# Column-normalised attention followed by a top-1 mixture of experts: three spare half units behind a run-time branch

## The chip, the cores and the metric

The kernel runs on one core of a Trainium2 chip. The metric is the device time of one execution in microseconds (us), as the median of several runs. A separate execution under the hardware profiler gives the trace from which all rows below come. The engines are TensorE (PE; its weight loads are listed apart as PEld), VectorE (DVE), ScalarE (ACT), GpSimd (POOL) and SyncE (SP); POOL issues the indirect DMAs here and SP the direct ones. A `q` behind an engine's name (POOLq) is its sequencer.

## What is computed

For each of 4 batches `q`, `k`, `v` are 5056 x 256. The columns of `q` and `k` are normalised over the 5056 rows, a 256 x 256 matrix is formed from them and put through a softmax, and `v` is multiplied with it. The 20,224 rows that result are the tokens of a mixture of 8 experts with one expert for each token:

```python
qn = q / (norm(q, axis=1) + 1e-6);  kn = k / (norm(k, axis=1) + 1e-6)
a = softmax(kn.transpose(0, 2, 1) @ qn / tau)
x = (v @ a).reshape(B * S, D)
e_idx = argmax(x @ w_gate, axis=1)
for e in range(E):
    mask = e_idx == e
    h = maximum(x[mask] @ w1[e], 0)
    out[mask] = gate_w[mask] * eom[mask, e] * (h @ w2[e])
```

How many tokens each expert gets is known only at run time.

## The kernel before

**Stages.** `gram` (L306) builds the 256 x 256 matrix of a batch, `mix` (L434) multiplies `v` with it, `route` (L494) finds each token's expert and scatters the token into that expert's region of a DRAM buffer `xs_d`, and `blocks` (L895) runs the experts' two layers over units of rows gathered from `xs_d`. `prep` and `split` (L236, L260) write each expert's weights to DRAM as a high and a low float16 part (`wsc`), from which units fetch them. These generators are woven into one another by `_beside` (L27); the instruction order on each engine follows from that order and from the framework's scheduler.

**Units.** A full unit has 256 rows (`BLK`, `nt = 2`), a half unit 128 (`nt = 1`). All units have rows of one expert. The number of units is fixed when the kernel is built (L77 to L86): `EARLY` = 10 full units from the first three batches, `LATER` = 62 more full ones, and `NHALF` = 21 halves, which is what the worst split of the tokens over the experts needs; `NUNIT` = 93. Before the first 10 and before the other 83, `checkpoint` (L724) has DVE work out from the counts which expert and which rows each unit has: `table` (L614) writes them into `elist`, `used` (1 where the unit has rows) and `gi` (the gather's indices), `weights` (L681) writes `wi`, the index by which a unit fetches weights. A unit without rows gathers 128 filler rows whose output index lies out of bounds, so that its store moves nothing; its `wi` is out of bounds too. Its matrix work is done all the same, since the instructions are the same for any data.

**Order of the units.** 10 early full units, then `lead` = `LATER` - `NHALF` = 41 full ones (units 10 to 50), then 21 pairs of a full unit and a half (units 51 to 92). So half number h is unit 52 + 2h, and the last three halves are units 88, 90 and 92, with full units 87, 89 and 91 between them. Halves are filled from the front: those without rows are the last.

**A step of `blocks`.** In step g the first layer of unit g (`h_part`, L837: for each half of a quarter 6 matmuls, 48 in all, with 256 columns for a full unit and 128 for a half) alternates with the second layer of unit g-1 (`y_part`, L860: 48 matmuls of 256 columns for a full unit, 24 for a half), in quarters h0 y0 h1 y1 h2 y2 h3 y3. After a quarter of h, ACT (L854) and DVE (L855) make its float16 parts; after the last quarter of y, ACT scales the result (L879) into `yo`. POOL fetches the two weight matrices into `wbuf[0]` and `wbuf[1]` (`fetch_w`, L768), each of which has two buffers that units take in turn (`u % NW`), gathers rows (`fetch_x`, L781) up to 6 units ahead, and stores one row block of 128 per instruction (`store`, L885). `prepare` (L792) scales and splits the rows on DVE and ACT and transposes them by a DMA on SP (L831). Two units that follow each other in the same buffer with the same expert need no new weights: `wi` is then out of bounds.

**End.** After the last step comes `store(NUNIT - 1)`; what the framework adds behind it (drains and semaphores) has L982.

Of the kernel before, what the change touches and what calls it, by code (L numbers as in the profile page):

```python
# [13 lines left out]
I32 = mybir.dt.int32  # L14
# [7 lines left out]
BLK = 256  # L22
# [4 lines left out]
def _beside(main, *others):  # L27

    due = [0.0 for _ in others]
    for _ in main:  # L30
        for i, (gen, rate) in enumerate(others):
            due[i] += rate
            while due[i] >= 1.0:
                due[i] -= 1.0
                next(gen, None)
# [3 lines left out]
def tile_colnorm_attention_then_top1_moe(  # L39
# [12 lines left out]
    nc = tc.nc  # L52
    B, N, C = q.shape
    E = w_gate.shape[1]
    FF = w1.shape[2]
    NTOK = B * N
# [20 lines left out]
    EARLY = 10  # L77
    LATER = (NTOK - E * (BLK - 1) + BLK - 1) // BLK - EARLY
    NHALF = (NTOK - (EARLY + LATER) * BLK + E * (BLK // 2 - 1)) // (BLK // 2)
# [4 lines left out]
    FIRST = [-(-r * SURE // E) for r in range(E)]  # L84
    assert EARLY <= FIRST[2] and EARLY + LATER - NHALF >= FIRST[E - 1]
    NUNIT = EARLY + LATER + NHALF  # L86
    QM = max(LATER, NHALF)
    NW = 2

    cst = ctx.enter_context(tc.tile_pool(name="cst", bufs=1))  # L90
# [32 lines left out]
    units = []  # L123
# [16 lines left out]
    def iota_f(shape, pattern, base, mult, name):  # L140
        ti = one.tile([P, shape], I32, tag="iota_i", name=name + "_i")
        nc.gpsimd.iota(ti, pattern=pattern, base=base, channel_multiplier=mult)
        tf = cst.tile([P, shape], F32, name=name)
        nc.vector.tensor_copy(tf, ti)
        return tf
# [8 lines left out]
    eoff = iota_f(E, [[CAP, E]], 0, 0, "eoff")  # L154
    jf = iota_f(QM, [[1, QM]], 0, 0, "jf")
    real = cst.tile([P, 1], F32, name="real")
# [32 lines left out]
    ri = cst.tile([P, E], I32, name="ri")  # L189
    elist = cst.tile([P, NW + NUNIT], F32, name="elist")  # L190
    nc.vector.memset(elist, -1.0)
# [11 lines left out]
    def grouped(ins, group, why):  # L203
        tc.declare_no_dep(ins.ins, group=group, reason=why)
        tc.add_to_no_dep_group(group, ins.ins)
# [30 lines left out]
    def prep(first, end, tag):  # L236
        todo = []
        for r in range(first, end):
            for half in range(2):
                if tag == "st":  # L240
                    raw = wk.tile([P, R, CW], F32, tag="st", name=f"raw{r}_{half}", bufs=STB)
                    raw = raw.rearrange("p r w -> p (r w)")[:, :HW1]
                else:
                    raw = big.tile([P, HW1], F32, tag="raw", name=f"raw{r}_{half}", bufs=3)
                nc.gpsimd.indirect_dma_start(
                    out=raw,
                    out_offset=None,
                    in_=wraw[half],
                    in_offset=bass.IndirectOffsetOnAxis(ap=ri[:, r : r + 1], axis=0),
                    bounds_check=E * P - 1,  # L250
                    oob_is_err=False,
                )
                todo.append(lambda raw=raw, half=half, r=r: split(raw, half, r))
                yield
                if len(todo) > 1:
                    yield from todo.pop(0)()
        for f in todo:
            yield from f()
# [171 lines left out]
    def finish(gen):  # L430
        for _ in gen or ():
            pass
# [137 lines left out]
    def open_marks(ck):  # L570
        nc.gpsimd.dma_start(mark[:, ck : ck + 1], xs_d[NSLOT:, 0:1])
# [37 lines left out]

    gi = cst.tile([P, NUNIT], I32, name="gi")  # L610
    wi = cst.tile([P, NUNIT], I32, name="wi")
    used = cst.tile([P, NUNIT], F32, name="used")

    def table(ck, unit, Q, places):  # L614

# [65 lines left out]
    def weights(a, b):  # L681

        ok = sm.tile([P, NUNIT], F32, tag="tb_ok", name="tb_ok")[:, a:b]
        now = elist[:, NW + a : NW + b]
        nc.vector.tensor_tensor(out=ok, in0=now, in1=elist[:, a:b], op=ALU.is_equal)
        nc.vector.tensor_tensor(out=ok, in0=ok, in1=used[:, a:b], op=ALU.is_ge)
        row = sm.tile([P, NUNIT], F32, tag="tb_wt", name="tb_wt")[:, a:b]
        nc.vector.tensor_scalar(out=row, in0=now, scalar1=float(P), scalar2=pidx, op0=ALU.mult, op1=ALU.add)
# [4 lines left out]
    def of_rank(dst, src):  # L693
        pr = sm.tile([P, E, E], F32, tag="tb_rk", name="tb_rk")
        nc.vector.tensor_tensor(out=pr, in0=rank, in1=src.unsqueeze(1).to_broadcast([P, E, E]), op=ALU.mult)
        nc.vector.tensor_reduce(out=dst, in_=pr, axis=AX.X, op=ALU.add)
# [27 lines left out]
    def checkpoint(last):  # L724
        if last:
            close_regions()
        else:
            rank_experts()
        of_rank(rcr, rc)
        open_marks(int(last))  # L730
        yield
        if not last:
            table(int(last), BLK, EARLY, lambda a: [(a[:, :EARLY], lambda r: r)])
            weights(0, EARLY)
            new = [2] * EARLY
        else:

            s = 1
            lead = LATER - s * NHALF
            mid = EARLY + lead  # L740

            def fulls(a):
                grid = a[:, mid:].rearrange("p (h s) -> p h s", s=s + 1)
                return [
                    (a[:, EARLY:mid], lambda r: r[:, :lead]),
                    (grid[:, :, :s], lambda r: r[:, lead:].rearrange("p (h s) -> p h s", s=s)),
                ][not lead :]

            def halves(a):
                grid = a[:, mid:].rearrange("p (h s) -> p h s", s=s + 1)  # L750
                return [(grid[:, :, s], lambda r: r)]

            table(int(last), BLK, LATER, fulls)
            table(int(last), BLK // 2, NHALF, halves)
            weights(EARLY, NUNIT)
            new = [2] * lead + ([2] * s + [1]) * NHALF
        for nt in new:
            u = len(units)
            units.append(dict(nt=nt, gi=gi[:, u : u + 1], wi=wi[:, u : u + 1], top=max(r for r in range(E) if FIRST[r] <= u)))
# [5 lines left out]
    def fetch_w(half, u):  # L765
        end = (units[u]["top"] + 1) * P
        assert len(prepped) * P >= end
        nc.gpsimd.indirect_dma_start(  # L768
            out=wbuf[half][:, u % NW, :],
            out_offset=None,  # L770
            in_=wsc[half][:end, :],
            in_offset=bass.IndirectOffsetOnAxis(ap=units[u]["wi"], axis=0),
            bounds_check=end - 1,
            oob_is_err=False,
        )
# [106 lines left out]
    def store(u):  # L882
        un = units[u]
        for t in range(un["nt"]):
            ins = nc.gpsimd.indirect_dma_start(  # L885
                out=out[:, :],
                out_offset=bass.IndirectOffsetOnAxis(ap=un["id"][:, t : t + 1], axis=0),
                in_=un["yo"][:, t, :],
                in_offset=None,
                bounds_check=NTOK - 1,  # L890
                oob_is_err=False,
            )
            grouped(ins, "out", "each token has an output row of its own")

    def blocks():  # L895

        got = dict.fromkeys(("w1", "w2", "x", "prep"), 0)

        def adv(stage, step, n):
            for u in range(got[stage], min(n, len(units))):  # L900
                step(u)
                got[stage] = u + 1

        g = 0
        while g <= NUNIT:
            while g < NUNIT and g + 1 > len(units):
                yield
            adv("w1", lambda u: fetch_w(0, u), g + NW - 1 if g else NW)
            adv("w2", lambda u: fetch_w(1, u), g + NW - 1)
            adv("x", fetch_x, got["prep"] + QKB)  # L910
            if g > 1:
                store(g - 2)
            if g == 0:
                yield
            adv("prep", prepare, g + 1)
            if g < NUNIT:
                hb = big.tile([P, HW1], F32, tag="raw", name="hb", bufs=3)
                units[g]["h"] = hb.bitcast(F16).rearrange("p (a f m) -> p a f m", a=2, f=FC)
            for fp, steps in enumerate(ORDER):
                for kind, part in steps:  # L920
                    if kind == "h" and g < NUNIT:
                        h_part(g, part)
                    if kind == "y" and g > 0:
                        y_part(g - 1, part)
                if fp == 1:
                    adv("prep", prepare, g + 1 + XP)
                yield
            g += 1
        store(NUNIT - 1)


    grams = [gram(b) for b in range(B)]
# [3 lines left out]
    for _ in grams[0]:  # L936
        for _ in range(PER_STAGE):
            next(ahead)
    run = blocks()
    for b in range(B - 1):  # L940
        _beside(mix(b), (ahead, GRATE))
    early = checkpoint(False)
# [11 lines left out]
    _beside(tail, (run, BRATE))  # L954
    finish(checkpoint(True))
    _beside(run, (prep(2, E, "st"), WRATE))


# [28 lines left out]
```

## Time and profile before

| what | value |
|---|---|
| median of 3 runs | 1265.51 us (1261.57 to 1273.47) |
| the profiled execution's own time | 1272.18 us |
| its span, first to last instruction | 1270.5 us |
| PE busy | 1204.7 us, 95% of the span |
| DVE, ACT, POOL busy | 735.6, 629.5, 655.8 us |
| mean granted clock of TensorE | 0.98 of full speed |

Busy time counts an engine's instructions; the rows in the section below are of one execution, with times in us from the start of its span. The profiled execution's own time is 1.7 us above its span, and lies 6.7 us above the median of the three runs.

### The profile page before, as it was taken

How to read it: one execution, taken by the hardware profiler on the slowest of the kernel's cores; microseconds unless marked ns; L12 is line 12 of the kernel's file. 1: busy time of each engine (PE TensorE's matmuls, PEld its weight loads, DVE VectorE, ACT ScalarE, POOL GpSimd, SP SyncE). 2: the span in 40 equal slices, each digit the busy share in tenths (PEclk: the TensorE clock that was granted, in tenths of full speed). 3: DMA queues.
4: the chain of work that ended last, by engine and by line, in shares of the span. 5: the costliest groups of instructions: out<-in, count | busy, mean ns of one | idle time of the engine just before them, and what ended most of it. 6: DMA issues, size and time to landing. Idle time of an engine off the chain costs nothing.

```text
span 1270.5 us, 28599 instructions
## 1 busy us (share of the span) xinstructions
PE 1204.7 (95%) x10708; PEld 1092.5 (86%) x10708; DVE 735.6 (58%) x2235; ACT 629.5 (50%) x1231; POOL 655.8 (52%) x643
## 2 busy tenths in 40 slices
PE   7999999996669999999999999899999999999996
PEld 6899898995668788888888888788899999999996
DVE  5767767766678466565656666444445555555431
ACT  4676666664755456455554645333333444334332
POOL 0005665667577754555555544344455555555442
PEclk9999999998879999999999999999999999999999
DMA  9877787857697765565565546933263333465520
GB/s 333 277 251 243 244 276 230 270 179 228 218 329 181 190 159 167 120 143 144 144 143 144 143 111 159 180 70 73 64 176 107 78 78 79 114 212 165 161 59 17
DMA packets 176418, 211.46 MB, mean 166 GB/s; under 512 B 125352, under 2 KB 127022, under 8 KB 171032
## 3 DMA queue, kind: packets, MB, share of 16 engines
q1 hardware_dynamic: 124568, 100.73, 29.4%
q0 software_dynamic: 51712, 108.92, 29.3%
q8 instruction: 84, 1.38, 0.5%
q14 instruction: 54, 0.44, 0.1%
HBM read 296.94 MB, written 61.80 MB: 282 GB/s over the span
## 4 chain that ended last, share of the span: by engine, by line
PE 81%; DMA 9%; DVE 3%; ACT 2%; issue 2%; POOL 1%; SPq 0%; POOLq 0%; ACTq 0%; DVEq 0%
PE h_ps L850 10%; PE h_ps L852 10%; PE h_ps L851 10%; PE y_ps L875 10%; PE y_ps L873 10%; PE y_ps L874 10%; PE s_ps L341 9%; DMA qk<-in_k_dram 3%; PE x_ps L479 3%; PE x_ps L480 2%; PE x_ps L481 2%; DMA xg<-xs_d,gi 2%; PE vt_ps L456 2%; DMA xs_d<-st,r_si 1%; DMA raw<-in_moe_w_dram,ri 1%
## 5 line engine op out<-in xcount | busy, mean ns | idle before, releaser
L850 PE MATMUL h_ps<-xt,wbuf 128*128 128x256 f16 (+1 forms) x1488 | 376.5, 262 | 7.4 <-DMA wbuf<-wsc,wi 5.2
L851 PE MATMUL h_ps<-xt,wbuf 128*128 128x256 f16 (+1 forms) x1488 | 376.5, 262 | 0.0
L852 PE MATMUL h_ps<-xt,wbuf 128*128 128x256 f16 (+1 forms) x1488 | 376.4, 262 | 0.0
L855 DVE SCALAR_TENSOR_TENSOR hb<-h_ps,hb 128x512 f16<-128x512 f32 (+1 forms) x372 | 232.3, 628 | 238.4 <-ACT hb L854 237.1
L875 PE MATMUL y_ps<-wbuf,hb 128*128 128x256 f16 x1320 | 360.1, 273 | 5.0 <-DVE hb L855 5.0
L873 PE MATMUL y_ps<-wbuf,hb 128*128 128x256 f16 x1320 | 360.0, 273 | 0.8 <-ACT hb L854 0.8
L874 PE MATMUL y_ps<-wbuf,hb 128*128 128x256 f16 x1320 | 360.0, 273 | 0.0
L854 ACT ACTIVATE hb<-h_ps 128x512 f16<-128x512 f32 (+1 forms) x372 | 199.7, 545 | 314.3 <-PE h_ps L852 310.6
L768 POOL DMA_INDIRECT wbuf<-wsc,wi x186 | 188.1, 1011 | 290.3 <-PE h_ps L852 242.4
L559 POOL DMA_INDIRECT xs_d<-st,r_si x160 | 177.0, 1106 | 194.8 <-ACT st L482 119.3
L885 POOL DMA_INDIRECT out_dram<-yo,b_id x165 | 168.4, 1021 | 60.4 <-issue 43.9
L850 PEld LDWEIGHTS <-wbuf 128*128 128x128 f16 x1488 | 147.1, 99 | 23.0 <-DMA wbuf<-wsc,wi 7.7
L851 PEld LDWEIGHTS <-wbuf 128*128 128x128 f16 x1488 | 146.2, 98 | 14.4
L341 PE MATMUL s_ps<-qk 128*128 128x256 f32 x640 | 150.3, 385 | 8.5 <-DMA qk<-in_k_dram 7.8
L852 PEld LDWEIGHTS <-wbuf 128*128 128x128 f16 x1488 | 146.3, 98 | 13.8
L875 PEld LDWEIGHTS <-hb 128*128 128x128 f16 x1320 | 129.2, 98 | 20.6 <-DVE hb L855 5.6
L874 PEld LDWEIGHTS <-hb 128*128 128x128 f16 x1320 | 129.2, 98 | 14.9 <-issue 0.9
L873 PEld LDWEIGHTS <-hb 128*128 128x128 f16 x1320 | 129.3, 98 | 14.0
L341 PEld LDWEIGHTS s_ps<-qk 128*128 128x128 f32 x640 | 119.5, 193 | 23.4 <-DMA qk<-in_q_dram 8.2
L826 ACT ACTIVATE xr<-xg,b_sx 128x256 f16<-128x256 f32 x165 | 75.6, 500 | 99.1 <-DMA xt<-xr 69.9
L329 DVE TENSOR_TENSOR acc<-acc,sq 128x1024 f32<-128x1024 f32 x76 | 93.0, 1224 | 52.4 <-ACT sq L328 43.8
L827 DVE SCALAR_TENSOR_TENSOR xr<-xg,b_sx,xr 128x256 f16<-128x256 f32 x165 | 74.0, 481 | 84.2 <-ACT xr L826 80.5
(187 smaller groups left out, 1603.8 us busy)
## 6 DMA issues: line engine op xcount, KB each, us to landing
qk<-in_q_dram SPq DMA_DIRECT2D x76, 256.0 KB
qk<-in_k_dram SPq DMA_DIRECT2D x76, 256.0 KB
v<-in_v_dram SPq DMA_DIRECT2D x32, 512.0 KB
wsc<-whi SPq DMA_DIRECT2D x16, 512.0 KB
wsc<-wlo SPq DMA_DIRECT2D x16, 512.0 KB
v<-in_v_dram SPq DMA_DIRECT2D x8, 480.0 KB
wbuf<-wsc,wi POOLq DMA_INDIRECT x186
xt<-xr SPq DMA_TRANSPOSE x165
```

Of the source, the lines that this page charges most:

```text
L341: nc.tensor.matmul(s_ps[:, c, :], kt[:, 1, t, c * P : (c + 1) * P], qt[:, 0, t, :], start=st == 0 and t0 == 0 and t == 0 and c == 0 and n ...
L559: ins = nc.gpsimd.indirect_dma_start(out=xs_d[:, :], out_offset=bass.IndirectOffsetOnAxis(ap=si[:np_, t : t + 1], axis=0), in_=st[:np_, t, ...
L768: nc.gpsimd.indirect_dma_start(out=wbuf[half][:, u % NW, :], out_offset=None, in_=wsc[half][:end, :], in_offset=bass.IndirectOffsetOnAxis( ...
L850: nc.tensor.matmul(hp, w1s[:, 0, c, fs], xh, start=fi == 0 and c == 0, stop=False, **KWM)
L851: nc.tensor.matmul(hp, w1s[:, 0, c, fs], xl, start=False, stop=False, **KWM)
L852: nc.tensor.matmul(hp, w1s[:, 1, c, fs], xh, start=False, stop=fin, **KWM)
L854: nc.scalar.activation(hh, h_ps[:, :, :w], AF.Relu)
L855: nc.vector.scalar_tensor_tensor(out=hb[:, 1, 2 * fp : 2 * fp + 2, :w], in0=h_ps[:, :, :w], scalar=0.0, in1=hh, op0=ALU.max, op1=ALU.subtract,
L873: nc.tensor.matmul(y_ps[:, t, :], hb[:, 0, f, tsl], w2s[:, 0, f, :], start=st, stop=False, **KWM)
L874: nc.tensor.matmul(y_ps[:, t, :], hb[:, 0, f, tsl], w2s[:, 1, f, :], start=False, stop=False, **KWM)
L875: nc.tensor.matmul(y_ps[:, t, :], hb[:, 1, f, tsl], w2s[:, 0, f, :], start=False, stop=fin, **KWM)
L885: ins = nc.gpsimd.indirect_dma_start(out=out[:, :], out_offset=bass.IndirectOffsetOnAxis(ap=un["id"][:, t : t + 1], axis=0), in_=un["yo"][ ...
```

## The change

`TAIL` = 3 of the 21 halves are taken out of the pairs. The units are now 10 early full ones, `lead` = 62 - 18 = 44 full ones (to unit 53), 18 pairs of a full unit and a half (units 54 to 89), and the three halves as units 90 to 92. `checkpoint` copies `used` of unit 90 into a new integer word `more_i`. `blocks` gets the first and the last unit as arguments; the main run covers units 0 to 89. After it every engine reads `more_i` into a register, and the steps of units 90 to 92 stand in a block that runs only if the word is above 0. Within that block the steps start anew: they share no step with unit 89.

```diff
+    TAIL = NHALF - max(0, (NTOK - (EARLY + LATER) * BLK + E * BLK // 4) // (BLK // 2))
+    assert 0 < TAIL < E
...
+    more_i = cst.tile([1, 1], I32, name="more_i")
...
-            s = 1
-            lead = LATER - s * NHALF
-            mid = EARLY + lead
+            few = NHALF - TAIL
+            lead = LATER - few
+            mid, end = EARLY + lead, NUNIT - TAIL
+
+            def pairs(a):
+                return a[:, mid:end].rearrange("p (h s) -> p h s", s=2)
 
             def fulls(a):
...
+                return [(a[:, EARLY:mid], lambda r: r[:, :lead]), (pairs(a)[:, :, 0], lambda r: r[:, lead:])]
 
             def halves(a):
-                grid = a[:, mid:].rearrange("p (h s) -> p h s", s=s + 1)
-                return [(grid[:, :, s], lambda r: r)]
+                return [(pairs(a)[:, :, 1], lambda r: r[:, :few]), (a[:, end:], lambda r: r[:, few:])]
...
             weights(EARLY, NUNIT)
-            new = [2] * lead + ([2] * s + [1]) * NHALF
+            nc.vector.tensor_copy(more_i, used[0:1, end : end + 1])
+            new = [2] * lead + [2, 1] * few + [1] * TAIL
...
-    def blocks():
+    def blocks(a, z):
 
-        got = dict.fromkeys(("w1", "w2", "x", "prep"), 0)
+        got = dict.fromkeys(("w1", "w2", "x", "prep"), a)
...
-            for u in range(got[stage], min(n, len(units))):
+            for u in range(got[stage], min(n, len(units), z)):
...
-        store(NUNIT - 1)
+        store(z - 1)
...
-    run = blocks()
+    run = blocks(0, NUNIT - TAIL)
...
+    more = nc.values_load(
+        more_i, min_val=0, max_val=1, skip_runtime_bounds_check_because="written as a comparison's result"
+    )
+    with tc.If(more > 0):
+        finish(blocks(NUNIT - TAIL, NUNIT))
```

Within `blocks` the bounds 0 and `NUNIT` become `a` and `z` throughout.

## Rows read from the trace of the kernel before

**Rows 1.** Page: busy us of each engine, share of the span, instructions

```profile
PE 1204.7 (95%) x10708; PEld 1092.5 (86%) x10708; DVE 735.6 (58%) x2235; ACT 629.5 (50%) x1231; POOL 655.8 (52%) x643
```

**Rows 2.** Windows: us, busy of PE, PEld, DVE, ACT, POOL; clock, DMA share, GB/s

```profile
1100.00:1150.00 50.00, 50.00 (x531) 45.65 (x529) 24.88 (x90) 19.42 (x44) 29.41 (x30) 1.00 0.69 207
...
1240.00:1270.00 30.00, 20.12 (x212) 18.09 (x209) 4.89 (x9) 6.93 (x15) 9.01 (x9) 0.92 0.06 18
```

**Rows 3.** Waits of PE, 800 to 1271: total us, times, longest

```profile
PE y_ps L875 <- DVE hb L855: 4.2, 1, 4.2
PE y_ps L873 <- ACT hb L854: 0.8, 1, 0.8
```

**Rows 4.** Timeline of PE, unit 92: start, us, instruction

```profile
1255.36 0.22 PE L850 MATMUL h_ps<-xt,wbuf 128*128 128x128 f16 x1
...
1256.03 0.27 PE L873 MATMUL y_ps<-wbuf,hb 128*128 128x256 f16 x1
...
1257.34 0.27 PE L873 MATMUL y_ps<-wbuf,hb 128*128 128x256 f16 x1
...
1259.85 0.27 PE L875 MATMUL y_ps<-wbuf,hb 128*128 128x256 f16 x1
```

**Rows 5.** Timeline of ACT: scaling of a full unit's output, two pairs

```profile
1241.76 0.84 ACT L879 ACTIVATE yo<-y_ps,b_gs 128x256 f32<-128x256 f32 x2 [0.93 <-PE y_ps L875]
...
1257.54 0.84 ACT L879 ACTIVATE yo<-y_ps,b_gs 128x256 f32<-128x256 f32 x2 [0.93 <-PE y_ps L875]
```

**Rows 6.** Timeline of POOL: stores of the halves 88, 90 and 92

```profile
1236.08 1.03 POOL L885 DMA_INDIRECT out_dram<-yo,b_id  x1 [0.30 <-issue]
...
1251.20 1.00 POOL L885 DMA_INDIRECT out_dram<-yo,b_id  x1 [0.31 <-DVE hb L855]
...
1260.95 0.97 POOL L885 DMA_INDIRECT out_dram<-yo,b_id  x1 [0.40 <-ACT yo L879]
```

**Rows 7.** Windows of 2 us behind stores of halves and of a full unit

```profile
1236.00:1238.00 2.00, 2.00 (x29) 1.86 (x26) 0.42 (x1) 0.38 (x1) 1.03 (x1) 1.00 0.09 9
...
1244.00:1246.00 2.00, 2.00 (x21) 1.80 (x19) 0.73 (x2) 0.60 (x1) 1.33 (x2) 1.00 0.20 70
...
1250.00:1252.00 2.00, 2.00 (x28) 1.86 (x26) 0.71 (x2) 0.48 (x2) 1.69 (x2) 1.00 0.03 0
```

**Rows 8.** Timeline of POOL: two weight fetches, the second for unit 86

```profile
1201.86 1.04 POOL L768 DMA_INDIRECT wbuf<-wsc,wi  x1 [3.58 <-PE h_ps L852]
...
1203.21 1.01 POOL L768 DMA_INDIRECT wbuf<-wsc,wi  x1 [0.31 <-PE h_ps L852]
```

**Rows 9.** Windows of 2 us: unit 86's second weight matrix arrives

```profile
1206.00:1208.00 2.00, 2.00 (x26) 1.87 (x25) 0.00 (x0) 0.00 (x0) 0.00 (x0) 1.00 0.98 389
...
1208.00:1210.00 2.00, 2.00 (x27) 1.85 (x26) 0.00 (x0) 0.46 (x2) 0.88 (x1) 1.00 0.36 139
```

**Rows 10.** The framework's end: instructions, min/median/max ns, first and last start

```profile
L982 SPq EVENT_SEMAPHORE  x11: 17/28/28, 1263.0 to 1270.4; - x11
...
L982 POOLq DRAIN  x3: 45/102/8963, 1260.7 to 1270.2; - x3
```

**Rows 11.** Timelines of DVE and POOL: unit index written, next weight fetch

```profile
414.19 0.24 DVE L689 SCALAR_TENSOR_TENSOR wi<-tb_ok,tb_wt 128x83 int32<-128x83 f32 x1
...
421.64 1.00 POOL L768 DMA_INDIRECT wbuf<-wsc,wi  x1 [0.31 <-issue]
```

**Rows 12.** Page: queues that fetch instructions (packets, MB, share of 16 engines)

```profile
q8 instruction: 84, 1.38, 0.5%
...
q14 instruction: 54, 0.44, 0.1%
```

**Rows 13.** Windows: the one stretch after 500 with an idle PE

```profile
800.00:820.00 20.00, 15.02 (x123) 12.50 (x122) 8.05 (x22) 6.73 (x15) 7.08 (x7) 0.91 1.06 178
```

**Rows 14.** Chain of waits, 300 to 900: start, us, what

```profile
336.95 3.59 DMA xg<-xs_d,gi
...
780.07 7.36 DMA xt<-xr
```

More of the change, by code (lines that the diff above doesn't have):

```diff
@@ L736, in checkpoint @@
         else:
-            s = 1
-            lead = LATER - s * NHALF
-            mid = EARLY + lead
-            def fulls(a):
-                grid = a[:, mid:].rearrange("p (h s) -> p h s", s=s + 1)
[L744 to L747, printed above, removed]
+            few = NHALF - TAIL
[3 more added lines that the diff above has]
+                return a[:, mid:end].rearrange("p (h s) -> p h s", s=2)
+            def fulls(a):
+                return [(a[:, EARLY:mid], lambda r: r[:, :lead]), (pairs(a)[:, :, 0], lambda r: r[:, lead:])]
             def halves(a):
-                grid = a[:, mid:].rearrange("p (h s) -> p h s", s=s + 1)
-                return [(grid[:, :, s], lambda r: r)]
+                return [(pairs(a)[:, :, 1], lambda r: r[:, :few]), (a[:, end:], lambda r: r[:, few:])]
             table(int(last), BLK, LATER, fulls)
@@ L893, in store @@
             grouped(ins, "out", "each token has an output row of its own")
-    def blocks():
-        got = dict.fromkeys(("w1", "w2", "x", "prep"), 0)
+    def blocks(a, z):
+        got = dict.fromkeys(("w1", "w2", "x", "prep"), a)
         def adv(stage, step, n):
-            for u in range(got[stage], min(n, len(units))):
+            for u in range(got[stage], min(n, len(units), z)):
                 step(u)
                 got[stage] = u + 1
-        g = 0
-        while g <= NUNIT:
-            while g < NUNIT and g + 1 > len(units):
+        g = a
+        while g <= z:
+            while g < z and g + 1 > len(units):
                 yield
-            adv("w1", lambda u: fetch_w(0, u), g + NW - 1 if g else NW)
+            adv("w1", lambda u: fetch_w(0, u), g + NW - 1 if g > a else g + NW)
             adv("w2", lambda u: fetch_w(1, u), g + NW - 1)
             adv("x", fetch_x, got["prep"] + QKB)
-            if g > 1:
+            if g > a + 1:
                 store(g - 2)
-            if g == 0:
+            if g == a:
                 yield
             adv("prep", prepare, g + 1)
-            if g < NUNIT:
+            if g < z:
                 hb = big.tile([P, HW1], F32, tag="raw", name="hb", bufs=3)
@@ L920, in blocks @@
                 for kind, part in steps:
-                    if kind == "h" and g < NUNIT:
+                    if kind == "h" and g < z:
                         h_part(g, part)
-                    if kind == "y" and g > 0:
+                    if kind == "y" and g > a:
                         y_part(g - 1, part)
```

## Prediction, made before the change was run

> **What bounds the kernel now.** I read the page's busy times first: PE is busy 95% of the span, no other engine above 58% [rows 1]. That is a mean over stages, so the stage that the change touches comes next. In the windows of the last part PE is busy 50.00 of 50 us at a granted clock of 1.00, while DVE, ACT and POOL are at 50 to 59% and the DMA queues at 0.69 [rows 2]; from 800 to the end PE waited twice, 5.0 us in all [rows 3], and both waits lie in one window at 800 to 820 [rows 13], among full units. So in the stretch of pairs PE never waits: a unit taken out there is worth its PE time, and a unit that only moves costs nothing. Behind the last matmul there is a second stage that PE does not bound: PE's last start is 1259.85 [rows 4], POOL's last store starts at 1260.95 [rows 6], and then comes the framework's end, whose longest piece is a drain on POOL of 8.96 us [rows 10].
>
> **Do the last three halves have rows?** The change gains only if units 88, 90 and 92 of before are empty, for they hold what units 90 to 92 hold after. A store with rows shows in the DMA: the two stores of full unit 89 give 70 GB/s in their window, but behind the store of unit 90, which starts at 1251.20, the window shows 0 GB/s, and behind that of unit 88, which starts at 1236.08, 9 GB/s, that is 18 KB in 2 us [rows 6, 7]. 18 KB is about one instruction packet (1.38 MB / 84 = 16 KB [rows 12]), where 128 rows of 1 KB are 131 KB. Unit 88 is the first of the three and decides, and since halves are filled from the front, 90 and 92 follow it. Counting the tokens in the reference gives the same: 10,076 and 9,709 for two experts, 33 to 180 for the six others, which makes 72 full units and 18 halves. So `more_i` is 0 and the block is jumped over.
>
> **The change part by part.**
>
> *Removed: three halves.* One quarter of a half's first layer takes 1256.03 - 1255.36 = 0.67 us, four take 2.68. Its second layer runs from 1257.34 to 1259.85 + 0.11 = 2.62 us [rows 4]. Together 5.30 us. Against it: two scalings of a full unit's output lie 1257.54 - 1241.76 = 15.78 us apart, which is one pair [rows 5]; less 5.30 that leaves 10.48 for the full unit, or 0.109 us for each of its 96 matmuls, as it should be. Three halves: -15.90 us. Their gathers, splits, transposes, weight fetches (which move nothing) and stores on the other engines lie beside PE now and give nothing.
>
> *Moved: halves start three units later.* Full units 10 to 50 become 10 to 53, and halves take the odd buffer of `wbuf` instead of the even one. The number of weight changes stays, two steps of 7.9 us still lie between a half and the next, and PE is covered throughout [rows 2, 3]: 0. One place loses its cover. The last half with rows had three more pairs behind it; now it is the last unit, and its second layer starts with no quarter of another unit's first layer ahead of it, 1.31 us earlier. In the trace that half is unit 86: its second matrix is fetched at 1203.21 [rows 8], the queues run at 389 GB/s until 1208 and at 139 after it [rows 9], so it has landed by about 1209, and its step ends at 1210.0. The fetch ahead of it on POOL, 1.04 us and a gap of 0.31 [rows 8], is for the next unit; that one is now in the block, so unit 86's fetch goes out 1.35 us earlier. Bounds 0 and +1 us; I take 0.
>
> *Added at the checkpoint.* `halves` now has two places instead of one, which is three more small DVE operations, and the copy to `more_i` is a fourth; none is longer than the 0.24 us of the operation that writes `wi`. That one starts at 414.19, and the first fetch that POOL begins after it starts at 421.64 with POOL busy until then [rows 11]. So 7 us of POOL's scatters hide them: 0; if that cover were gone, 4 x 0.24 = 1.0 us.
>
> *Added at the end: register reads and the jump.* PE, DVE and ACT are through before POOL's last store starts at 1260.95, since it stores what they made [rows 6]; behind the read their sequencers have only the end queued. The word was written some 830 us earlier [rows 11], so nobody waits for it. On POOL the read stands behind the last store and ahead of the 8.96 us drain, so POOL's part may be added in full. No row shows a register read or a jump. From below: 0, if the drain is a wait for something that runs on regardless. From above: the framework closes the branch as it closes the program, with a second drain and the barrier behind it, from 1260.7 to 1270.4 = 9.7 us [rows 10]. I take 1.2 us: the nearest rows are one DMA instruction of POOL, 0.97 us [rows 6], and some ten semaphore operations of at most 0.028 us [rows 10]. The last store has rows now; it lands within the drain.
>
> A rule that speaks against the change: what instruction loading costs here is seen as 84 packets on one queue at 0.005 x 16 x 1270.5 / 84 = 1.21 us each [rows 12], all beside other work. The Trainium skill (Runtime: NRT & Kernel Launch, Instruction fetch mechanics) says that a taken branch whose target lies outside the two pages held breaks the sequential prefetch and waits for a fetch. No jump stands in the trace. By the rule the sum would have another fetch on it; it is the first rival below. The skill's figures for branches alone (Advanced Engine Details and Errata, Control Flow Timing: about 51 ns, and 108 ns with a comparison) would make the estimate of the jump about 0.2 us instead of 1.2.
>
> **Sum.** Against the profiled execution's own time: 1272.18 - 15.90 + 1.2 = 1257.5 us. That execution lies 6.7 us above the median of the three runs, with no sign in the trace that the end stage is the reason, so I take the same 14.7 us off the median: 1265.51 - 14.7 = 1250.8, rounded to 1251 us, or -1.2%. A measurement of this kernel can tell about 1% from no change, here 12.7 us: the forecast is only 2 us beyond that.
>
> **Rivals** (on the median's scale).
>
> *The jump waits for instructions on POOL.* PE jumps over the most code, but it is idle from 1260 to 1270 anyway; only POOL's (or SP's) jump lies on the path. For: no operation of before tests it. Against: POOL skips about a dozen DMA instructions, little code. Price: a small DMA to its landing, 3.59 us [rows 14], and a packet's 1.21: +4.8. 1250.8 + 4.8 = 1255.6 us, -0.8%.
>
> *A second closing sequence.* For: the semaphores that the skipped block would have raised have to be squared on both ways through, and a full stop is the simple means. Against: semaphore operations alone do that at 0.03 us each. Price: 9.7 in place of 1.2: 1259.3 us, -0.5%.
>
> *The new order shifts a stall.* PE idles 5 us at 800 to 820, where the DMA queues show 1.06 [rows 13]; the shifted halves could bring one such meeting of weight loads and gathers more, or one less. Against: this place lies at full units whose order does not change, and the loads of halves cost PE nothing now. Price 5 us either way: 1255.8 or 1245.8 us.
>
> *The block is run: slower than before.* If the first of the three has so much as one row, units 90 to 92 run after the main run with nothing ahead: a gather (about 1.0 to issue, as in rows 6, and 3.59 to land [rows 14]), a split of about 2 us, a transpose of 3 to 7 [rows 14] (weights land meanwhile), 10 to 14 us of idle PE, with the three halves' 15.9 us paid as before. 1265.5 + 1.2 + 12 = 1279 us, +1.0%. It decides at the first row in unit 90, and rows 7 speak against it.
>
> **How the numbers follow.** Forecast 0.62, waiting for instructions 0.10, second closing 0.12, a stall more 0.08, a stall less 0.05, block run 0.03. The forecast's 1251 stands. Faster by over 1% means below 1252.9: about 0.85 of the forecast (jump under 3.2 us), the stall less, and a little of the rest: 0.59. Slower by over 1%: half of the last rival, 0.02. Within 1%: 0.39. The range: below, one stall less and a little beyond, 1244; above, the second closing, 1260. Within the forecast alone, with the jump between 0 and 3 us and the medians' own spread, 1247 to 1255.
>
> **What would show it.** Right: 3 x (48 + 24) = 216 fewer matmuls on PE, and 12 fewer DMA instructions on POOL (six weight fetches, three gathers, three stores); PE's last matmul at about 1244 us of the span; the pairs again 15.78 us apart with PE at 100%; from PE's last matmul to the end of the span 10.4 us plus at most 3. Wrong in the jump: a second long drain or a gap on POOL ahead of the end. Wrong in the order: a wait of PE for `wbuf` among the pairs or ahead of the last second layer. The whole forecast falls if units 90 to 92 show matmuls.

## The result, and the profile after

The changed kernel takes 1252.89 us (median of 20 runs) against 1267.38 us for the kernel before (20 runs): a ratio of 0.9886, 95% interval 0.9871 to 0.9902, or 14.4 us less. One of the changed kernel's 20 runs, 1267.73 us, was in a slower state and is left out of the ratio. The forecast was 1251 us, 14.7 us less. The profiled execution took 1251.43 us, with a span of 1249.7.

In the changed kernel's file the lines stand three further down: L853 to L855 are the first layer's matmuls, L876 to L878 the second's, L882 the scaling, L888 the store; L961 is the read of `more_i`, L964 the branch, L991 what the framework adds at the end.

Busy times of the page [rows 1] and windows among the pairs and at the earlier stall [rows 2, 13], of the kernel after:

```profile
PE 1186.9 (95%) x10492; PEld 1077.2 (86%) x10492; DVE 726.1 (58%) x2197; ACT 623.5 (50%) x1213; POOL 640.2 (51%) x631
```

```profile
1100.00:1150.00 50.00, 50.00 (x537) 45.70 (x535) 26.27 (x96) 19.80 (x44) 29.39 (x29) 1.00 0.54 144
800.00:820.00 20.00, 18.53 (x170) 16.21 (x168) 10.81 (x33) 6.18 (x14) 8.09 (x9) 1.00 0.89 140
```

PE has 10,492 matmuls where it had 10,708: 216 fewer, so units 90 to 92 were not computed. Among the pairs PE is busy 50.00 of 50 us as before, and the old stall at 800 to 820 is down from 5.0 us to 1.5. The waits of PE from 800 to the end [rows 3] and ACT's scalings of the last units [rows 5]:

```profile
PE y_ps L876 <- DMA wbuf<-wsc,wi: 1.2, 1, 1.2
PE y_ps L878 <- DVE hb L858: 0.3, 1, 0.3
```

```profile
1217.59 0.84 ACT L882 ACTIVATE yo<-y_ps,b_gs 128x256 f32<-128x256 f32 x2 [0.93 <-PE y_ps L878]
...
1233.37 0.84 ACT L882 ACTIVATE yo<-y_ps,b_gs 128x256 f32<-128x256 f32 x2 [0.93 <-PE y_ps L878]
1236.04 0.47 ACT L882 ACTIVATE yo<-y_ps,b_gs 128x256 f32<-128x256 f32 x1 [1.83 <-issue]
```

Both waits of PE lie in the window at 800 to 820, so among the pairs and behind them PE never waited. Two full units' scalings lie 1233.37 - 1217.59 = 15.78 us apart, as before. The last half's scaling comes 1236.04 - 1233.37 = 2.67 us behind that of the last full unit. In the kernel before the last scaling, of an empty half, lies as far behind that at 1257.54 [rows 5]:

```profile
1260.21 0.47 ACT L879 ACTIVATE yo<-y_ps,b_gs 128x256 f32<-128x256 f32 x1 [1.83 <-issue]
```

So the second layer of the last half did not wait for its weights.

What the removal was worth can be read without the noise of the earlier stages. Both orders have the same units up to 50, so POOL's first store of unit 49 is a common mark. In the kernel before that store is

```profile
925.08 1.02 POOL L885 DMA_INDIRECT out_dram<-yo,b_id  x1 [0.30 <-issue]
```

and the last store is at 1260.95 [rows 6]: 335.87 us. In the changed kernel the same two stores are

```profile
916.81 1.03 POOL L888 DMA_INDIRECT out_dram<-yo,b_id  x1 [0.30 <-issue]
...
1236.79 0.97 POOL L888 DMA_INDIRECT out_dram<-yo,b_id  x1 [0.41 <-ACT yo L882]
```

319.98 us apart: 15.89 us less, where the prediction had 15.90. From the start of the last store to the end of the span it was 1270.5 - 1260.95 = 9.55 us; now it is 1249.7 - 1236.79 = 12.91. So the end has grown by 3.36 us, and here is where. These are PE's last matmul and sequencer instructions of the kernel after (of the latter min/median/max in ns, first and last start in us), which answer to [rows 10]:

```profile
1235.68 0.27 PE L878 MATMUL y_ps<-wbuf,hb 128*128 128x256 f16 x1
...
L961 POOLq TENSOR_LOAD <-more_i x1: 688/688/688, 1236.6 to 1236.6; - x1
...
L964 POOLq EVENT_SEMAPHORE  x4: 17/43/2149, 1237.8 to 1240.1; - x4
...
L964 PEldq COMPARE_BRANCH  x1: 1045/1045/1045, 1234.4 to 1234.4; - x1
...
L964 ACTq COMPARE_BRANCH  x1: 50/50/50, 1236.6 to 1236.6; - x1
...
L964 POOLq COMPARE_BRANCH  x1: 45/45/45, 1237.3 to 1237.3; - x1
L964 POOLq INC_SWDGE_SEM  x1: 1840/1840/1840, 1240.2 to 1240.2; - x1
...
L991 POOLq DRAIN  x3: 45/107/6770, 1242.1 to 1249.4; - x3
```

POOL's store ends at 1237.76. POOL's sequencer then stands at a semaphore until about 1240.0 (the longest of four, 2.149 us), adds to the semaphores of the DMAs that the jump has left out (`INC_SWDGE_SEM`, 1.840 us from 1240.2; called the squaring below), and only at 1242.1 begins the closing drain. That drain is shorter than before, 6.77 us against 8.96, but begins 4.3 us behind the end of the last store, where it began beside that store before. POOL's read (0.69 us) falls beside the issue of the last store, and its jump takes 0.045 us. ACT's jump takes 0.050 us; PE's takes 1.05, at a time when its last matmuls have been handed on; they run until 1235.8.

The sum over the trace: -15.89 + 3.36 = -12.5 us. The ratio says -14.4, with an interval of -16.3 to -12.4. The other 2 us, if they are not noise, must lie ahead of unit 49. The two profiles cannot tell: they differ by 8.3 us there (925.08 against 916.81), and of that 3.5 us are the stall of the kernel before at 800 to 820 [rows 13].

### The profile page after: what moved, and what is told of

It reads as the page before. It is cut to its first block, busy times and chain, and to the rows that moved or that the text cites. A ratio compares the mean times of both kernels' runs of the same rounds, so it can differ in the third digit from the quotient of the medians.

```text
span 1249.7 us, 28075 instructions
## 1 busy us (share of the span) xinstructions
PE 1186.9 (95%) x10492; PEld 1077.2 (86%) x10492; DVE 726.1 (58%) x2197; ACT 623.5 (50%) x1213; POOL 640.2 (51%) x631
## 4 chain that ended last, share of the span: by engine, by line
PE 82%; DMA 8%; issue 4%; POOL 2%; ACT 2%; DVE 2%; SPq 0%; POOLq 0%; ACTq 0%; DVEq 0%
PE h_ps L853 10%; PE h_ps L855 10%; PE h_ps L854 10%; PE y_ps L876 10%; PE y_ps L878 10%; PE y_ps L877 10%; PE s_ps L344 9%; PE x_ps L482 3%; PE x_ps L483 3%; PE x_ps L484 3%; PE vt_ps L459 2%; DMA wbuf<-wsc,wi 2%; DMA qk<-in_k_dram 2%; DMA xt<-xr 1%; DMA raw<-in_moe_w_dram,ri 1%
## 5 line engine op out<-in xcount | busy, mean ns | idle before, releaser
L853 PE MATMUL h_ps<-xt,wbuf 128*128 128x256 f16 (+1 forms) x1440 | 367.4, 263 | 8.1 <-DMA wbuf<-wsc,wi 4.9
L854 PE MATMUL h_ps<-xt,wbuf 128*128 128x256 f16 (+1 forms) x1440 | 367.2, 263 | 0.0
L855 PE MATMUL h_ps<-xt,wbuf 128*128 128x256 f16 (+1 forms) x1440 | 367.2, 263 | 0.0
L858 DVE SCALAR_TENSOR_TENSOR hb<-h_ps,hb 128x512 f16<-128x512 f32 (+1 forms) x360 | 227.4, 635 | 232.7 <-ACT hb L857 228.0
L876 PE MATMUL y_ps<-wbuf,hb 128*128 128x256 f16 x1296 | 353.3, 273 | 1.2 <-DMA wbuf<-wsc,wi 1.2
L878 PE MATMUL y_ps<-wbuf,hb 128*128 128x256 f16 x1296 | 353.3, 273 | 0.3 <-DVE hb L858 0.3
L877 PE MATMUL y_ps<-wbuf,hb 128*128 128x256 f16 x1296 | 353.3, 273 | 0.0
L857 ACT ACTIVATE hb<-h_ps 128x512 f16<-128x512 f32 (+1 forms) x360 | 195.4, 550 | 309.0 <-PE h_ps L855 305.1
L771 POOL DMA_INDIRECT wbuf<-wsc,wi x180 | 182.3, 1013 | 285.0 <-PE h_ps L855 237.6
L562 POOL DMA_INDIRECT xs_d<-st,r_si x160 | 174.2, 1089 | 193.7 <-ACT st L485 117.7
L888 POOL DMA_INDIRECT out_dram<-yo,b_id x162 | 166.0, 1025 | 64.6 <-issue 42.7
L853 PEld LDWEIGHTS <-wbuf 128*128 128x128 f16 x1440 | 142.2, 99 | 22.2 <-DMA wbuf<-wsc,wi 5.7
L854 PEld LDWEIGHTS <-wbuf 128*128 128x128 f16 x1440 | 141.3, 98 | 15.3 <-issue 1.3
L855 PEld LDWEIGHTS <-wbuf 128*128 128x128 f16 x1440 | 141.3, 98 | 13.6
L877 PEld LDWEIGHTS <-hb 128*128 128x128 f16 x1296 | 126.8, 98 | 15.2 <-issue 1.4
L878 PEld LDWEIGHTS <-hb 128*128 128x128 f16 x1296 | 126.8, 98 | 15.2 <-DVE hb L858 0.5
L876 PEld LDWEIGHTS <-hb 128*128 128x128 f16 x1296 | 126.9, 98 | 13.9
```

The costliest lines, as they stand in the source:

```text
L562: ins = nc.gpsimd.indirect_dma_start(out=xs_d[:, :], out_offset=bass.IndirectOffsetOnAxis(ap=si[:np_, t : t + 1], axis=0), in_=st[:np_, t, ...
L771: nc.gpsimd.indirect_dma_start(out=wbuf[half][:, u % NW, :], out_offset=None, in_=wsc[half][:end, :], in_offset=bass.IndirectOffsetOnAxis( ...
L853: nc.tensor.matmul(hp, w1s[:, 0, c, fs], xh, start=fi == 0 and c == 0, stop=False, **KWM)
L854: nc.tensor.matmul(hp, w1s[:, 0, c, fs], xl, start=False, stop=False, **KWM)
L855: nc.tensor.matmul(hp, w1s[:, 1, c, fs], xh, start=False, stop=fin, **KWM)
L857: nc.scalar.activation(hh, h_ps[:, :, :w], AF.Relu)
```

## Experiments

Three questions were open: whether the longer end belongs to the branch, what in the branch costs it, and where the last 2 us come from. Ratios are to the kernel before on the same chip, with their 95% intervals. PE's end is the start of its last matmul plus 0.11 us; from there to the end of the span it was 1270.5 - 1259.96 = 10.5 us before [rows 4], and is 1249.7 - 1235.79 = 13.9 in the changed kernel.

### No block at all

```diff
-    more = nc.values_load(
...
-    with tc.If(more > 0):
-        finish(blocks(NUNIT - TAIL, NUNIT))
```

The copy to `more_i` goes with it.

> The changed kernel without the register reads, the branch and the block: units 90 to 92 are left out altogether (they have no rows with these inputs). Theory A (the new order is worth nothing, the branch costs 3.4 us behind the last store): three halves less, 15.9 us, so a ratio of about 0.9875 to the kernel before, and the stretch from the start of POOL's last store to the end of the span is 9.5 us as before, against 12.9 in the changed kernel. Rival B (the new order itself is worth about 2 us, which is what the changed kernel gained beyond 15.9 - 3.4): ratio about 0.986, pairs or the stretch ahead of them shorter. Rival C (the branch costs nothing, the longer end of the changed kernel is chance): the last stretch is 12.9 us here too.

Measured: 0.9835 (0.9805 to 0.9865). POOL's last store and its closing drain (the store is L887 in this file, the end L984):

```profile
1238.43 0.97 POOL L887 DMA_INDIRECT out_dram<-yo,b_id  x1 [0.41 <-ACT yo L881]
...
L984 POOLq DRAIN  x3: 45/102/7983, 1238.2 to 1246.7; - x3
```

The stretch behind the last store is 1247.1 - 1238.43 = 8.7 us, 0.9 less even than before: the drain is 7.98 us here. Unit 49's first store to the last store: 319.97 us, as in the changed kernel. So C falls: the long end goes with the block, and against this kernel the branch costs 12.9 - 8.7 = 4.2 us. Neither A nor B had the shorter end, and A's ratio of 0.9875 lies outside the interval. The ratio shows 21 us less than before (17 to 25; the medians, 1246.05 against 1265.37, 19.3), where 15.9 and 0.9 make 16.8. So here too some us more are gone than the trace shows behind unit 49.

### The new order alone

```diff
-    run = blocks(0, NUNIT - TAIL)
+    run = blocks(0, NUNIT)
```

and no copy, reads or block behind it.

> The new order of units (44 full ones, 18 pairs, three halves) in one run with no branch: all 93 units are computed. Theory A: the same work at the same speed, ratio 1.000 within the noise, the last stretch 9.5 us. Rival B (the order is worth about 2 us): ratio about 0.9985; as that is within what five rounds can tell, the trace decides: PE idle between the first half unit and the last matmul, which A puts at 0 to 1 us in both orders.

Measured: 0.9988 (0.9968 to 1.0007), last stretch 9.54 us. PE did not wait once from 830 us on. From unit 49's first store to the last it takes 1251.96 - 916.08 = 335.88 us, the old order 335.87. The order is worth nothing from unit 49 on, as A says; B's 2 us are within the interval, but not in the pairs.

### One half in the block

```diff
-    TAIL = NHALF - max(0, (NTOK - (EARLY + LATER) * BLK + E * BLK // 4) // (BLK // 2))
+    TAIL = 1
```

> TAIL set to 1: only the last half stands in the block, the two other spare halves stay in pairs. Theory A with a fixed price: -5.3 + 3.4 = -1.9 us, ratio 0.9985, the last stretch 12.9 us. Theory A with a price that grows with the DMA instructions jumped over (4 instead of 12): the counting-up instruction on POOL, 1.84 us with 12, is about 0.6, the last stretch about 11.6, ratio 0.9975. Rival C (no price): -5.3 us, 0.996, last stretch 9.5.

Measured: 0.9970 (0.9942 to 0.9998). PE's last matmul, POOL's last two stores, the branch's semaphores and squaring, and PE's waits from 830 on:

```profile
1253.06 0.27 PE L878 MATMUL y_ps<-wbuf,hb 128*128 128x256 f16 x1
...
1252.78 0.98 POOL L888 DMA_INDIRECT out_dram<-yo,b_id  x1 [0.30 <-issue]
1255.95 0.97 POOL L888 DMA_INDIRECT out_dram<-yo,b_id  x1 [2.19 <-DMA out_dram<-yo,b_id]
...
L964 POOLq EVENT_SEMAPHORE  x2: 17/30/43, 1252.9 to 1253.0; - x2
...
L964 POOLq INC_SWDGE_SEM  x1: 1981/1981/1981, 1253.1 to 1253.1; - x1
...
PE h_ps L853 <- DVE hb L858: 0.7, 1, 0.7
PE y_ps L876 <- ACT yo L882: 0.3, 1, 0.3
```

The squaring takes 1.98 us with 4 DMA instructions jumped over, 1.84 with 12, so the guess that it grows in proportion to their number (0.6 us with 4) falls. That it is a fixed price is not shown: with 4 its first 0.66 us lie beside the store that ends at 1253.76, and may be a wait for it. The semaphore waits are 0.043 us at most. Here POOL meets the branch between its last two stores, so the last store goes out late, at 1255.95, 2.8 us behind PE's end at 1253.17, where it was 1.0 us before. From PE's end to the end of the span it is 12.0 us, against 10.5 before and 13.9 in the changed kernel: a price of 1.5 us. With 5.3 less for the half that makes -3.8 us, as the ratio says (-7.3 to -0.3). The stretch from the start of the last store, 1265.2 - 1255.95 = 9.25 us, looks like rival C's 9.5, but only because that store itself is late. In this profile itself PE's end lies only 4.0 us nearer to unit 49's first store (922.28) than before, since PE waited 0.7 and 0.3 us on the way. No expectation had the branch ahead of the last store.

### A branch without DMAs

The kernel before with the copy to `more_i`, the reads and a branch over one DVE instruction; no unit is left out.

```diff
+    more = nc.values_load(
...
+    with tc.If(more > 0):
+        nc.vector.memset(spare, 0.0)
```

> The kernel before, in its old order with all 93 units, and at its end the five register reads and a branch over a block that holds one memset on DVE and no DMA. Theory A (the price is that POOL has to square the semaphores of the DMAs in the jumped block, and first waits for its own last store): without DMAs in the block POOL has the read of 0.69 us and the branch of 0.05 ahead of its drain, the drain ends when it did, and the last stretch is 9.5 to 10.3 us; ratio 1.000 to 1.0006. Rival D (any branch costs this, whatever the block holds): last stretch 12.9 us, ratio 1.0027.

Measured: 0.9969 (0.9947 to 0.9991), 4 us less than before, which neither expectation had. It told nothing on the end, since the framework had moved the block, which depends on nothing: POOL's jump is at 415 us.

```profile
L964 POOLq COMPARE_BRANCH  x1: 45/45/45, 415.1 to 415.1; - x1
```

So the block was tied to the last unit:

```diff
-        nc.vector.memset(spare, 0.0)
+        nc.vector.tensor_copy(spare, units[NUNIT - 1]["yo"][:, 0, 0:1])
```

> The kernel before with the reads and the branch over a block of one DVE copy that reads the last unit's output tile, so that it can only stand at the end (the bare branch without that landed at 410 us). Theory A (the price is POOL's squaring of the jumped DMAs and its wait for the last store): no such instruction on POOL, from PE's end to the end of the span 10.4 to 11.1 us, as against 13.8 in the changed kernel and 10.4 in the one before; ratio 1.000 to 1.0006. Rival D (any branch at the end costs that): 13.8 us, ratio 1.0027.

Measured: 0.9955 (0.9937 to 0.9972). PE's last matmul, and POOL's last store, read, jump and drain:

```profile
1250.12 0.27 PE L878 MATMUL y_ps<-wbuf,hb 128*128 128x256 f16 x1
...
1251.23 0.97 POOL L888 DMA_INDIRECT out_dram<-yo,b_id  x1 [0.40 <-ACT yo L882]
...
L961 POOLq TENSOR_LOAD <-more_i x1: 504/504/504, 1248.9 to 1248.9; - x1
...
L964 POOLq COMPARE_BRANCH  x1: 45/45/45, 1249.5 to 1249.5; - x1
...
L991 POOLq DRAIN  x3: 45/113/8963, 1251.0 to 1260.5; - x3
```

There is no squaring and no wait; the drain begins at 1251.0, beside the last store, and is 8.963 us long as in the kernel before. From PE's end to the end of the span: 10.6 us, where it was 10.5. D falls, and A holds: reads and jump cost nothing at the end; what costs is POOL's squaring for jumped DMAs and the wait ahead of it. But the whole kernel was 5.7 us faster than the one before, with all its work done and a branch added. No theory had that.

### Is it the branch, the build or chance?

The late bare branch has the same instructions in the same order as the kernel before, apart from the copy to `more_i`, the reads and the branch itself. Three controls: the kernel before once more; that kernel with the copy alone; the late bare branch once more.

```diff
+            nc.vector.tensor_copy(more_i, used[0:1, NUNIT - 1 : NUNIT])
```

> The kernel before, unchanged, as a control. Ratio 1.000. What it tells is in the trace: in the profile of before PE idles 55 us ahead of 900 us, 5.0 of them at 800 to 830, where the four other profiles so far show 49 to 52 in all. Theory E (that was one execution's chance; the order is the same up to the first half unit): about 49 to 52 us here, span about 1264. Rival (the old order stalls there): 5 us at 800 to 830 again.

> The kernel before with one more DVE operation, the copy of a used flag to more_i at the checkpoint, and nothing else: no reads, no branch, old order. Theory F (builds with the same work and the same order differ by some us ahead of the pairs, whatever the edit, which is where the changed kernel's last 2 us and the 6 us of the late bare branch come from): ratio anywhere from 0.995 to 1.000, and from POOL's store number 99 to its last one 335.9 us as in every 93-unit kernel in the old order. Rival G (the branch's presence makes the stretch ahead faster): 1.000 here, 0.9955 with a branch.

> The late bare branch once more, word for word, to see whether its 0.9955 holds. If it is a property of the build: 0.994 to 0.997 again. If it was the hour: 0.998 to 1.001.

Measured: 0.9993 (0.9969 to 1.0017) for the kernel before, 0.9975 (0.9941 to 1.0009) with the copy, 0.9947 (0.9915 to 0.9978) for the late bare branch. So its gain is a property of that kernel and not of the hour. The copy's interval holds what F and G expected alike. From unit 49's first store to the last it takes 335.87 us in the kernel before, its repeat (1256.77 - 920.90), the copy (1253.29 - 917.42) and the first profile of the late bare branch (1251.23 - 915.36); what these differ by lies ahead of that. The repeat of the late bare branch took 1258.88 - 921.05 = 337.83 us there, with one wait of PE among the pairs, so a single profile can stray there too:

```profile
PE h_ps L853 <- DVE hb L858: 1.8, 1, 1.8
```

The kernel before, run again, idles 53.1 us on PE ahead of 900, more than theory E's 49 to 52 and less than the 55 of its first profile. It does stall at 760 to 830, but by 1.4 us, not 5; the late bare branch does not stall there at all:

```profile
760.00:830.00 70.00, 68.62 (x631) 61.55 (x630) 40.72 (x113) 32.67 (x60) 34.69 (x34) 1.00 0.71 167
```

```profile
760.00:830.00 70.00, 70.00 (x645) 62.79 (x643) 41.70 (x110) 32.35 (x60) 33.28 (x32) 1.00 0.64 165
```

The 5 us of [rows 13] were in part one execution's chance. In all three profiles of a bare branch PE is busy 70.00 of these 70 us, and in the ten others of this case it idles 1.1 to 5.0 us, so a part of the gain may lie in this stall. A rule that any branch gains some 5 us (rival G) does not hold: for one half in the block the sum and the ratio agree, and for the kernel with own buffers, below, the ratio is some 3 us above its sum of -15.9 + 3.6; in both, 5 us less than the sum would lie outside the interval. What sets this part was not found.

### The block run

```diff
-            nc.vector.tensor_copy(more_i, used[0:1, end : end + 1])
+            nc.vector.tensor_copy(more_i, onesf[0:1, 0:1])
```

> The changed kernel with more_i set to 1, so that the block is run although its units have no rows; the output does not depend on it. Prediction's rival: 10 to 14 us of idle PE behind unit 89, 15.9 us for the halves as before, no squaring of semaphores on POOL: ratio about 1.005 to 1.012. Other view (POOL reaches the block while PE still works, so gathers and weights are there early): idle 4 to 7 us, ratio 1.001 to 1.004.

Measured: 1.0119 (1.0089 to 1.0148), slower. PE's wait between unit 89 and unit 90, and three windows there:

```profile
PE h_ps L853 <- DMA xt<-xr: 15.9, 1, 15.9
```

```profile
1240.00:1245.00 5.00, 0.00 (x0) 0.00 (x0) 0.00 (x0) 0.00 (x0) 3.78 (x5) 0.50 0.13 28
...
1250.00:1255.00 5.00, 2.90 (x28) 2.93 (x29) 1.25 (x5) 1.03 (x3) 0.00 (x0) 0.50 0.40 78
1255.00:1260.00 5.00, 5.00 (x73) 4.85 (x71) 2.12 (x5) 1.77 (x5) 0.99 (x1) 0.92 0.02 3
```

PE waits 15.9 us in one piece for the transposed rows, more than either expectation had. POOL issues its DMAs one every 1.3 us, and three weight fetches, from 1238.35 on, stand ahead of the first gather at 1242.31, which is 6.1 us behind the start of PE's wait at 1236.18; ACT splits that unit's rows at 1248.28, and PE starts behind the transpose at 1252.10. In that time the granted clock falls to 0.50, the lower of the two levels (1.2 GHz of 2.4), and it is still 0.50 when PE starts, so the halves take 17.7 us from PE's restart to its end instead of 15.9. If the tokens split so that unit 90 has rows, the change costs some 15 us instead of gaining 14. That is an estimate from this run, in which the three units had no rows and fetched no weights; with rows it was not run.

### Trying to hide the squaring

With one half in the block, POOL met the branch before its last store. To bring that about with three, the block's third unit got tiles of its own and the block fetched all its weights into the even buffer (the weight index of the block's first unit is compared with unit 89 here, which matters only where the block is run):

```diff
+                yo = one.tile([P, 2, C], F32, tag="at", name="yo_at")
...
+                un["y"] = ps_s.tile([P, 2, C], F32, tag="s", name="y_ps_s")
...
+                    hb = wk.tile([P, R, CW], F32, tag="st", name="hb_st", bufs=STB)
...
+        return u % NW if u < NUNIT - TAIL else (NUNIT - TAIL) % NW
```

> The changed kernel with buffers of its own for what the block's third unit shared with unit 89 (both weight fetches of the block go to the even buffer, its hidden activations, its output sum and its output tile to tiles that are free by then), so that POOL meets the branch before its last store instead of behind it. Theory A: POOL's wait for the last store's landing (2.15 us) is gone from the path, the squaring (1.84) is not: from PE's end to the end of the span 11.9 us, as with one half in the block, instead of 13.8; ratio about 0.9875 to 0.988 if the changed kernel is 0.9886 to 0.989. Rival: the wait comes again for the store ahead of the branch, 13 us or more, no gain.

Measured: 0.9924 (0.9891 to 0.9956). PE's last matmul, POOL's last two stores and the branch's instructions (in this file L911 is the store and L991 the branch):

```profile
1240.57 0.27 PE L898 MATMUL y_ps<-wbuf,hb 128*128 128x256 f16 x1
...
1240.30 0.98 POOL L911 DMA_INDIRECT out_dram<-yo,b_id  x1 [0.30 <-issue]
1246.21 0.97 POOL L911 DMA_INDIRECT out_dram<-yo,b_id  x1 [4.94 <-DMA wbuf<-wsc,wi]
...
L991 POOLq EVENT_SEMAPHORE  x4: 17/43/2767, 1240.4 to 1243.4; - x4
...
L991 POOLq INC_SWDGE_SEM  x1: 1820/1820/1820, 1243.5 to 1243.5; - x1
```

The rival was right: the wait came again, 2.77 us, now behind the store ahead of the branch, and the last store stood behind it and the squaring until 1246.21. From PE's end to the end of the span it is 14.1 us, against 13.9 in the changed kernel: no gain. The wait ends 3.1 us after the start of the store ahead of it, and in the two profiles of the changed kernel 3.2 and 3.0, as a wait for that store to land would; the trace names no releaser. With 4 jumped DMAs there was no such wait, which is not explained. No version was found that beats the changed kernel for any split of the tokens; the kernel with no block is faster, but right only where the last three halves are empty.

### The changed kernel again

> The changed kernel once more, beside the two others on the same chip. Ratio 0.987 to 0.990; from POOL's store number 99 to its last one 320.0 us, from the start of that store to the end of the span 12.9 us.

Measured: 0.9891 (0.9841 to 0.9942). Unit 49's first store and the last store:

```profile
914.62 1.03 POOL L888 DMA_INDIRECT out_dram<-yo,b_id  x1 [0.31 <-issue]
...
1234.60 0.97 POOL L888 DMA_INDIRECT out_dram<-yo,b_id  x1 [0.42 <-ACT yo L882]
```

319.98 us apart, and 1247.4 - 1234.60 = 12.8 us to the end, where the first profile had 319.98 and 12.9.

## Why the prediction held, and where it did not

**Whether the halves have rows.** Right: 216 matmuls and 12 of POOL's instructions fewer (631 against 643 on the page). The empty windows behind two stores [rows 7] decided it.

**The removal.** 15.90 us predicted, 15.89 measured between the two marks, and 15.9 in the repeat and without a block. In a stage where PE is busy 50.00 of 50 us each matmul taken out paid in full. One figure beside it is misread: ACT is busy 19.42 of these 50 us, 39% and not 50 to 59 [rows 2]; nothing rested on it.

**The moved halves.** Right at nothing: the order alone takes 335.88 us where the old one took 335.87, and the last half's weights were there in time.

**The checkpoint.** Four small operations with no loss seen: the three that come with the order stand in 0.9988 (0.9968 to 1.0007), the copy alone in 0.9975 (0.9941 to 1.0009). A loss of 1 us could hide in such intervals.

**The end.** Mis-sized: 1.2 us, measured 3.4 against the kernel before and 4.2 against the same kernel without a block. The sign set for it failed too: from PE's end to the end of the span the prediction allowed 10.4 us plus at most 3, and it is 13.9. The step that failed is the argument that semaphore operations of 0.028 us do the squaring. Here one instruction of 1.82 to 1.98 us did it for POOL's jumped DMAs, and with 12 of them POOL stood 2.0 to 2.8 us at a semaphore ahead of it. The bounds, 0 to 9.7, held it. The lower bound, a drain that waits for something that runs on regardless, falls: of the 7.98 us without a block 1.2 lie before the end of the last store (1239.40), which leaves 6.8, and in the changed kernel the drain takes 6.77 though it begins 4.3 us behind that store. The late start was paid in full.

**The rivals.** The second closing did not come: one long drain only. PE's jump took 1.05 us where ACT's and DVE's take 0.05 to 0.07, and 0.77 in the kernel with own buffers; PE's jump over one half took 0.23, over the bare block 0.23, and its branch 0.18 at most when the block is run. It cost nothing, since the end went through POOL. The longer jump agrees with the rule of the Trainium skill (Runtime: NRT & Kernel Launch, Instruction fetch mechanics) for the engine that jumps furthest; that the time went to a fetch is not shown. That the order shifts a stall is not seen: at 760 to 830 PE idles 5.0 us in one profile of the kernel before and 1.4 in the other, 2.8 and 1.5 in the changed kernel, and 1.1 with the order alone. The run block was named with 10 to 14 us of idle PE and came with 15.9; the part that its sum named, from the first gather on, took 9.8; what it lacked is the 6.1 us until POOL issues that gather, three weight fetches among them, and the lower clock, which cost 17.7 - 15.9 = 1.8 us. The forecast for it, +1.0%, came out as +1.2%.

**Why the total fits.** In part by luck: the end cost 2.2 us more than said, and by the ratio the changed kernel is some 2 us (0 to 4) faster than the trace accounts for, which no step predicted and no experiment explains.

## What to carry to other kernels

The stage in which PE never waited paid for every instruction removed from it (15.89 us of 15.90), so in such a stage size the removal by that engine's time between two marks that both kernels share; whole-span differences of two profiles (20.8 us here) carry several us that other stages differ by. The branch that jumped over POOL's DMAs made POOL settle their semaphores, with the wait ahead of it 4 us on the path, as POOL came last; a branch over compute alone cost nothing at the end. Before leaving work behind a branch, price the case in which it is taken: here some 15 us lost against 14 gained.

## What was not expected of the hardware

`INC_SWDGE_SEM` took 1.82 to 1.84 us for 12 jumped DMAs and 1.98 us for 4. Counted from the end of the last store, the closing drain on POOL took 7.7 to 7.8 us in kernels whose last store moves nothing (8.81 to 8.97 from the drain's start) and 6.8 where it has rows (7.98, or 6.77 when begun late); with one half in the block, where the last store moves nothing, it was 7.4. Why is open. Kernels with the same instructions in the same order, apart from a branch, differ by some 6 us (0.9955 and 0.9947 for the late bare branch, 0.9993 for the kernel before against itself), which is some 40% of what this change was worth; the traces put the difference ahead of unit 49.
